# One GpSimd library, exponentials parked in idle tiles, and three TensorE tile modes in the plan of a two-attention kernel

## Chip, cores and metric

The kernel runs on one core of one Trainium2 chip. The metric is device time in microseconds (us), the median of some runs of the same program.

## What is computed

Two independent attention layers, A (linear) and B (softmax), read inputs of their own; their outputs stand side by side in the last dimension. Batch is 1, S = 2048, D = 512, and there are H = 32 heads of Dh = 16. All inputs are bf16.

```python
# both: qkv = x @ wqkv, split into q, k, v of [32 heads, 2048, 16]
phi = lambda t: jnp.where(t > 0, t + 1, jnp.exp(t)) + 1e-6
# A
kv  = einsum("bhsd,bhse->bhde", phi(k), v);  z = einsum("bhsd->bhd", phi(k))
o   = einsum("bhqd,bhde->bhqe", phi(q), kv) / (einsum("bhqd,bhd->bhq", phi(q), z) + 1e-6)
# B
p   = softmax(einsum("bhqd,bhkd->bhqk", q, k) * Dh ** -0.5)
o   = einsum("bhqk,bhkd->bhqd", p, v)
# both: o.reshape(S, D) @ wo
```

B has 32 x 2048 x 2048 exponentials, and these fill the run.

## The kernel before

**Tiling of B.** The heads are taken in four groups of eight (`Gp`). A group's projections give `QT` and `KM` with the 8 x 16 head dimensions on the partitions, and `VV` with the keys on the partitions; each head's 16 columns of V are followed by a column of ones, so that the row sum comes with the product. `KM` is kept twice, with the even or the odd heads zeroed, so that 32 rows hold one live head. A *unit* is one group, 512 queries and one parity; there are 32. A unit has 64 *blocks*: 16 key tiles of 128 by four row groups `g`. A block's scores, 128 keys by 512 queries, fill one of TensorE's accumulator banks (`pS`, seven banks).

**Scores and products on TensorE.** A score matmul (L732) uses 32 of the 128 rows, at row position 32g, so that four blocks of different g run side by side. A product matmul (L1061, out `pPV`) uses 32 of the columns, at column position 32g, and again four run side by side; 17 of these columns are used. All other matmuls (projections L495 and L570, everything of A, output L680) use the whole array. These are three ways of cutting the array into tiles, called here row mode (q), column mode (p) and whole mode (w).

**Exponentials.** Two engines make them. ScalarE takes two or three blocks that lie in neighbouring banks with one ACTIVATE (L933). VectorE takes one or two (L828): it multiplies and adds so that the int16 result, read as f16, is a rough exponential. GpSimd then makes two shifted copies of it with `int64_add` (L1007), and the three weighted together are exact enough. So a block of VectorE costs TensorE three product matmuls, and a block of ScalarE one. Exponentials lie in `PT`, 46 buffers of 512 columns, until their product has run. After a unit VectorE transposes and normalises the result (L1081 to L1094) into one of 16 tiles of `ON`.

**A and the rest are jobs.** Each projection, each step of A and each output tile is a *job*: a list of stages on the engines, with one bank from `DSET` (three banks that the blocks of VectorE use as well). `bjobs` are B's projections for later groups, then the Gram matrices of x and of the weights and a flag (`gram_x`, `gram_w`, `flag_job`): they tell whether the scores could be too large, in which case a second, general program runs after this one. It is skipped with these inputs.

**Order.** All instructions are put in order while the program is built. A planner keeps an expected time `T` for each engine and picks the next item among candidates: a group of scores for ScalarE (`fill_act_cand`), scores for VectorE, a batch of products (`pv_cand`), a job's next stage. Items of ScalarE come first: another item goes on TensorE only if it ends before ScalarE would run dry (`lim`). `SW` = 0.1 us is added when the mode changes; before the change the planner knew two modes, row mode `"q"` and everything else `"w"`. Where TensorE would idle in the plan, `fill_in` puts in matmuls with zero weights (L1268), at 0.107 us each. `fill_act_cand` may also hold scores back until enough banks of `DSET` are free (`WAITN`), so that scores for VectorE ride in the same row-mode run.

```python
            if nfill[0] >= 2 and d_backlog(start) < DLOW and not lagging(start):
                late = T["act"] + sum(exps) - 0.222 - SW - LAT - WAITM
...
                if md != mode[0]:
                    st = max(st, T["pe"] + SW)
                    mode[0] = md
```

**Start.** GpSimd makes an identity matrix (`identb`, L369 and L370); TensorE needs it to transpose the first two tiles of x. GpSimd's `affine_select` and `int64_add` come from loadable libraries, and the compiler puts a load ahead of the first use of each.

## Time and profile before

| | |
|---|---|
| median of 3 runs | 719.79 us (717.92 to 721.84) |
| the profiled execution | 721.31 us; its span is 719.6 us |
| TensorE matmuls (PE) | 693.6 us busy, 96% of the span |
| ScalarE (ACT) | 686.8 us, 95% |
| VectorE (DVE) | 551.8 us, 77% |
| GpSimd (POOL) | 372.2 us, 52% |
| mean granted TensorE clock | 0.992 |

A busy time is the union of an engine's records. The records of successive instructions overlap by about a tenth of a microsecond, so an engine that reads 95% may still wait a little before each instruction; the distance from one start to the next tells more. "Idle" in a row is the engine's gap before the instruction, with the instruction that ended the wait behind the arrow.

### The profile page before, as it was taken

The numbers are of one execution on the slowest core, as the hardware profiler recorded it, in microseconds if no ns is written. First come the engines' busy times: TensorE is split into PE (matmuls) and PEld (weight loads), VectorE is DVE, ScalarE is ACT, GpSimd is POOL, SyncE is SP. The second block draws the span as 40 slices with busy tenths as digits, with TensorE's granted clock in tenths as the row PEclk, the third lists the DMA queues.
The fourth block names the chain that finished last, engine by engine and source line by source line (L and its number), as shares of the span: only waits on it lengthen the run. The fifth ranks groups of instructions, "written<-read, shape, count | busy, mean of one in ns | idle before, by whom it ended". The sixth has DMA issues, their size and how long they took to land.

```text
span 719.6 us, 16347 instructions
## 1 busy us (share of the span) xinstructions
PE 693.6 (96%) x6716; PEld 227.8 (32%) x6716; DVE 551.8 (77%) x912; ACT 686.8 (95%) x703; POOL 372.2 (52%) x633
## 2 busy tenths in 40 slices
PE   6899999999999999999999999999999999999996
PEld 4233333333333333332232322233243232223323
DVE  4696778777778876778987878878866787778771
ACT  3699999999999999999999999999999999999995
POOL 4455566444556554555554567534541465547560
PEclk9899999999999999999999999999999999999999
DMA  9900000000000000000010010000001001110001
GB/s 211 257 2 1 2 1 1 10 9 10 7 1 2 1 1 2 6 10 11 8 31 23 2 24 15 23 9 8 17 9 30 24 8 38 37 38 9 9 24 34
DMA packets 36578, 17.38 MB, mean 24 GB/s; under 512 B 27537, under 2 KB 35985, under 8 KB 36497
## 3 DMA queue, kind: packets, MB, share of 16 engines
q1 hardware_dynamic: 35408, 15.61, 8.9%
q8 instruction: 55, 0.90, 0.5%
q10 hardware_dynamic: 1088, 0.66, 0.3%
q14 instruction: 27, 0.21, 0.1%
HBM read 4.46 MB, written 4.19 MB: 12 GB/s over the span
## 4 chain that ended last, share of the span: by engine, by line
PE 72%; ACT 21%; DVE 4%; issue 2%; POOL 0%; ACTq 0%; DVEq 0%; POOLq 0%
PE pPV L1061 26%; PE pS L732 24%; ACT PT L933 20%; PE pS L680 4%; PE pS L495 4%; PE pS L601 3%; DVE PT L828 2%; PE pPV L1268 2%; PE pS L570 2%; PE pS L627 2%; ACT EA L592 1%; DVE OT L1081 1%; PE pS L650 1%; PE pS L618 1%; PE pS L529 1%
## 5 line engine op out<-in xcount | busy, mean ns | idle before, releaser
L933 ACT ACTIVATE PT<-pS 128x1024 f16<-128x1024 f32 (+1 forms) x665 | 672.4, 1126 | 14.3 <-PE pS L732 11.0
L1007 POOL INT64_ADD PT<-PT x608 | 364.8, 613 | 319.8 <-DVE PT L828 276.2
L828 DVE TENSOR_SCALAR PT<-pS 128x512 int16<-128x512 f32 (+1 forms) x550 | 380.8, 733 | 67.7 <-PE pS L732 61.4
L1061 PE MATMUL pPV<-PT,VV 128*17 128x512 f16 x3254 | 290.5, 385 | 2.8 <-DVE OT L1081 2.7
L732 PE MATMUL pS<-QT,KM 32*128 32x512 bf16 x2048 | 280.0, 386 | 8.1 <-ACT PT L933 3.7
L732 PEld LDWEIGHTS pS<-QT,KM 32*128 32x128 bf16 x2048 | 72.7, 91 | 238.5 <-ACT PT L933 149.0
L1061 PEld LDWEIGHTS pPV<-PT,VV 128*17 128x17 bf16 x3254 | 63.1, 88 | 127.4 <-issue 100.2
L601 PE MATMUL pS<-Wa,xTa 128*128 128x256 bf16 x256 | 41.3, 276 | 1.1 <-DVE PT L828 0.8
L1081 DVE STREAM_TRANSPOSE OT<-pPV 128x512 f32<-128x512 f32 x32 | 22.7, 710 | 23.4 <-PE pPV L1061 23.3
L495 PE MATMUL pS<-xTb,Wb 128*128 128x512 bf16 x120 | 38.2, 385 | 0.5 <-DVE PT L828 0.3
L1268 PE MATMUL pPV<-xTb,ZW 128*17 128x256 bf16 x206 | 34.7, 275 | 0.0
L473 DVE CAST KNa<-pS 128x512 bf16<-128x512 f32 x30 | 20.5, 685 | 13.5 <-PE pS L680 12.1
L601 PEld LDWEIGHTS pS<-Wa,xTa 128*128 128x128 bf16 x256 | 18.7, 97 | 22.8 <-issue 13.8
L680 PE MATMUL pS<-WOa,KNa 128*128 128x512 bf16 x64 | 20.9, 386 | 0.7 <-DVE PT L828 0.5
L593 DVE TENSOR_SCALAR EA<-EA 128x512 bf16<-128x512 bf16 x32 | 12.3, 383 | 11.6 <-ACT EA L592 11.5
L570 PE MATMUL pS<-Wb,xTb 128*128 128x128 bf16 x256 | 20.9, 221 | 0.2 <-DVE PT L828 0.2
L1268 PEld LDWEIGHTS pPV<-xTb,ZW 128*17 128x17 bf16 x206 | 16.5, 91 | 14.1 <-issue 9.1
L627 PE MATMUL pS<-xTa,Wa 128*128 128x512 bf16 x64 | 19.9, 384 | 0.9 <-DVE PT L828 0.8
L592 ACT ACTIVATE EA<-pS 128x512 bf16<-128x512 f32 x32 | 20.1, 629 | 0.0
L1089 DVE TENSOR_TENSOR OT<-OT,ZR 128x256 bf16<-128x256 f32 x32 | 17.8, 558 | 0.6
L570 PEld LDWEIGHTS pS<-Wb,xTb 128*128 128x128 bf16 x256 | 14.4, 98 | 10.4 <-issue 7.6
L680 PE MATMUL pS<-WOb,ON 128*128 128x512 bf16 x48 | 15.2, 385 | 0.0
(78 smaller groups left out, 221.0 us busy)
## 6 DMA issues: line engine op xcount, KB each, us to landing
out_dram<-KNa SPq DMA_DIRECT2D x30, 128.0 KB, 1.7
Wa<-in_A_wqkv_dram SPq DMA_DIRECT2D x1, 1536.0 KB, 7.1
KM<-KR SPq DMA_DIRECT2D x96, 16.0 KB, 1.8
Wb<-in_B_wqkv_dram SPq DMA_DIRECT2D x2, 384.0 KB, 4.4
Wb<-in_B_wqkv_dram SPq DMA_DIRECT2D x1, 512.0 KB, 4.7
WOb<-in_B_wo_dram SPq DMA_DIRECT2D x1, 512.0 KB, 7.9
WOa<-in_A_wo_dram SPq DMA_DIRECT2D x1, 512.0 KB, 8.8
ON<-in_B_x_dram ACTq DMA_DIRECT2D x1, 256.0 KB, 2.9
```

Source lines behind the costliest of these rows:

```text
L495: return e.matmul(f32v(bk), lhsT=Wb[:, cc, kind * 512 + Gp * 128:kind * 512 + Gp * 128 + 128], rhs=xTb[:, cc, sc * 512:(sc + 1) * 512], st ...
L570: return e.matmul(f32v(bk)[:, tl * 128:(tl + 1) * 128], lhsT=xTb[:, cc, t * 128:(t + 1) * 128], rhs=Wb[:, cc, 1024 + Gp * 128:1024 + Gp * ...
L601: return e.matmul(f32v(bk)[:, 256 * tt:256 * tt + 256], lhsT=xTa[:, cc, (t2 + tt) * 128:(t2 + tt + 1) * 128], rhs=Wa[:, cc, 512 * kind + 2 ...
L627: return e.matmul(f32v(bk), lhsT=Wa[:, cc, bq * 128:(bq + 1) * 128], rhs=xTa[:, cc, sc * 512:(sc + 1) * 512], start=(cc == 0), stop=(cc == 3))
L680: return e.matmul(f32v(bk), lhsT=src, rhs=WO[:, hb, :], start=(hb == 0), stop=(hb == 3))
L732: return e.matmul(dst, lhsT=KM[32 * g:32 * g + 32, Gp % 2, e_, j * 128:(j + 1) * 128], rhs=QT[32 * g:32 * g + 32, Gp % 2, c * 512:(c + 1) ...
L828: sch.add("dve", lambda e: e.tensor_scalar(PTi[:, i * 512:(i + n) * 512], PS[:, b0 * 512:(b0 + n) * 512], ESC, EB, op0=ALU.mult, op1=ALU.add),
L933: sch.add("act", lambda e: e.activation(PT[:, p0 * 512:p0 * 512 + w], PS[:, use[0] * 512:use[0] * 512 + w], ACTF.Exp, scale=SC), reads=[(" ...
L1007: sch.add("pool", lambda e: e.int64_add(PTl[:, pos * 128:pos * 128 + w], PTl[:, p0 * 128:p0 * 128 + w], v_), reads=[("PT", p0 + i) for i i ...
L1061: sch.add("pe", lambda e, g=g, j=j, hl=hl, pi=pi, k=k, first=first, last_=last_: e.matmul(PVb[32 * g:32 * g + 17, 0:512], lhsT=VV[:, Gp % ...
L1081: sch.add("dve", lambda e: e.transpose(OT[:, 0, :], PVb[:, 0:512]), reads=[("PV", g) for g in range(4)], writes=[("OT", 0)])
L1268: ins = e.matmul(dst, lhsT=ZW[:, 0:17], rhs=xTb[:, 0, 0:256], start=first, stop=first, tile_position=(0, 32 * g))
```

## The change

**One library.** A four-column memset and an `int64_add` of one element are put ahead of everything else on GpSimd, so that the library with `int64_add` is loaded first; `affine_select` then runs from it.

**Memory.** x and the weights of B, the `PT` buffers and `ON` become one tile, `MEM`, of 28 + 45 + 16 buffers. The 45 are free for exponentials from the start, and of the 16 output tiles all but the first four until shortly before their result is due (`EXP`). The 28 of x and weights open once the last projection of B and the flag are done; the Gram and flag jobs therefore move from the end of `bjobs` to its thirteenth place. The first write to such a buffer waits for all readers of what lay there (`parts`). The fillers read zeros instead of x. The general program loads x and the weights again; it does not run here.

**Planner.** Products get a mode of their own, `"p"`, so that `SW` is charged for every change between the three modes, in the start time and in the rule that protects ScalarE. A group of scores is held back until the third bank is expected free, with banks that VectorE has yet to empty estimated (`est_free`), and constants change.

```diff
@@ constants @@
-    NB = 46
+    NP = 45
+    EXP = 4
-    PVQ = 11
-    PVO = 12
-    RES = 8
-    WAITN = 2
+    PVQ = 9
+    PVO = 6
+    RES = 4
+    DLOW2 = 1.0
+    WAITN = 3
-    TEND = 670.0
+    TEND = 640.0
-    DBL = 3.0
-    DLOW = 1.5
+    DBL = 4.0
+    DLOW = 0.6
@@ memory @@
-        xTb = sb("xTb", [128, 4, S], BF)
+        X0, W0, P0 = 0, 16, 28
+        O0 = P0 + NP
+        NB = O0 + NT
+        PT = sb("MEM", [128, NB * 512], F16)
+        PTi, PTl, PTb = PT.bitcast(I16), PT.bitcast(I64), PT.bitcast(BF)
+        xTb = PTb[:, 0:W0 * 512].rearrange("p (c s) -> p c s", c=4)
+        Wb = PTb[:, W0 * 512:P0 * 512].rearrange("p (c n) -> p c n", c=4)
+        ON = PTb[:, O0 * 512:NB * 512].rearrange("p (t n) -> p t n", n=512)
...
-        ZW = sb("ZW", [128, 128], BF)
+        ZW = sb("ZW", [128, 256], BF)
@@ start of GpSimd @@
+        sch.add("pool", lambda e: e.memset(identb[:, 0:4], 0.0), writes=["identb"])
+        sch.add("pool", lambda e: e.int64_add(identb.bitcast(I64)[:, 0:1], identb.bitcast(I64)[:, 0:1], 0), reads=["identb"], writes=["identb"])
         mk_ident(identb, "identb")
@@ which buffers hold exponentials @@
-        ptfree = [0.0] * NB
+        ptfree = [0.0 if P0 <= i < O0 or i >= O0 + 4 else None for i in range(NB)]
+        retired = set(range(O0, O0 + 4))
+        for i in range(P0):
+            sch.parts[("PT", i)] = ([("xTb", t) for t in range(4 * (i % 4), 4 * (i % 4) + 4)] if i < W0 else
+                                    [("Wb", kd, g) for kd in range(2) for g in range(NGP)] + [("Wb", 2)])
...
+                    k_ = (u + EXP) // 2
+                    if 4 <= k_ < NT:
+                        retired.add(O0 + k_)
+                        ptfree[O0 + k_] = None
...
+            if not opened[0] and not bjobs and not early and all(t_ in tok for t_ in lastb):
+                opened[0] = True
+                for i in range(P0):
+                    ptfree[i] = T["pe"] + LAT
@@ fill_act_cand: when to hold a group of score blocks back @@
-                now = sum(bfree[x] is not None and bfree[x] <= start + 0.05 for x in DSET)
-                if now < WAITN:
-                    t1 = sorted(bfree[x] for x in DSET if bfree[x] is not None and start + 0.05 < bfree[x] <= late)
-                    if t1:
-                        start = t1[0]
+                est = sorted(est_free(x) for x in DSET)
+                if start + 0.05 < est[WAITN - 1] <= late:
+                    start = est[WAITN - 1]
...
-                if more and d_backlog(st) < DLOW:
+                if more:
                     ids = [x for x in DSET if bfree[x] is not None and bfree[x] <= st]
-                    if len(ids) <= 2 and d_pick(st + 0.05, ()) is not None:
+                    if d_backlog(st) < (DLOW, DLOW2, -1)[len(ids) - 1] and d_pick(st + 0.05, ()) is not None:
                         more = False
@@ gram and flag jobs @@
-        bjobs += [gram_x(i, ready=0) for i in range(4)] + [gram_w(i, ready=0) for i in range(2)] + [flag_job(ready=0)]
+        gj = [gram_x(i, ready=0) for i in range(4)] + [gram_w(i, ready=0) for i in range(2)] + [flag_job(ready=0)]
+        bjobs[12:12] = gj
@@ fillers @@
-                    ins = e.matmul(dst, lhsT=ZW[:, 0:17], rhs=xTb[:, 0, 0:256], start=first, stop=first, tile_position=(0, 32 * g))
+                    ins = e.matmul(dst, lhsT=ZW[:, 0:17], rhs=ZW[:], start=first, stop=first, tile_position=(0, 32 * g))
@@ the planner's mode of a candidate @@
-                opts.append((pc[0], pc[3], "pe", pc[1], pc[2], None, "w"))
+                opts.append((pc[0], pc[3], "pe", pc[1], pc[2], None, "p"))
...
-                keep = [o for o in opts if o[2] != "pe" or o[4] is fa[2] or o[0] + o[3] + (SW if mode[0] == "q" and o[6] == "w" else 0) <= lim]
+                keep = [o for o in opts if o[2] != "pe" or o[4] is fa[2] or o[0] + o[3] + (SW if mode[0] != o[6] else 0) <= lim]
```

What the compiler and the planner make of it, in the order in which instructions stand on an engine:

GpSimd at the start, before, from the identity matrix on (L370 ISA is a library load; `ZMk` is a small mask):

```order
L369 MEMSET identb 128x128
L370 ISA
L370 AFFINE_SELECT identb<-identb 128x128
L387 MEMSET ZMk 128x8
L388 AFFINE_SELECT ZMk<-ZMk 128x8
```

and before, the last masks and the first `int64_add` (L1007 ISA without a tile is the second load):

```order
L388 AFFINE_SELECT BMk<-BMk 128x128
L390 AFFINE_SELECT BMk<-BMk 128x128
L404 MEMSET VNa 128x32
L1007 ISA
L1007 ISA PT<-PT 128x512 x196
```

Now the only load (L385) stands ahead of the identity matrix:

```order
L384 MEMSET identb 128x4
L385 ISA
L385 ISA identb<-identb 128x2
L379 MEMSET identb 128x128
L380 AFFINE_SELECT identb<-identb 128x128
```

and the masks run into the additions without one:

```order
L400 AFFINE_SELECT BMk<-BMk 128x128
L402 AFFINE_SELECT BMk<-BMk 128x128
L416 MEMSET VNa 128x32
L1034 ISA MEM<-MEM 128x512 x66
L1034 ISA MEM<-MEM 128x256 x2
```

What moved: the second load is gone, and one memset and one addition stand ahead of the identity matrix.

TensorE, the twelve rows ahead of the first output matmul of A, before (L732 row mode, L1061 column mode, L650 whole mode, L1268 fillers):

```order
L732 MATMUL pS<-QT,KM 128x512 x3
L1061 MATMUL pPV<-PT,VV 17x512 x4
L650 MATMUL pS<-RHA,PQT 128x128 x4
L732 MATMUL pS<-QT,KM 128x512 x2
L650 MATMUL pS<-RHA,PQT 128x128 x4
L1061 MATMUL pPV<-PT,VV 17x512 x5
L732 MATMUL pS<-QT,KM 128x512 x3
L1061 MATMUL pPV<-PT,VV 17x512 x5
L732 MATMUL pS<-QT,KM 128x512 x4
L1061 MATMUL pPV<-PT,VV 17x512 x2
L1268 MATMUL pS<-xTb,ZW 17x256 x3
L732 MATMUL pS<-QT,KM 128x512 x4
```

and now (L744, L1088 and L662 are the same three kinds):

```order
L1088 MATMUL pPV<-MEM,VV 17x512 x8
L662 MATMUL pS<-RHA,PQT 128x128 x4
L744 MATMUL pS<-QT,KM 128x512 x4
L1088 MATMUL pPV<-MEM,VV 17x512 x16
L744 MATMUL pS<-QT,KM 128x512 x3
L1088 MATMUL pPV<-MEM,VV 17x512 x8
L744 MATMUL pS<-QT,KM 128x512 x5
L1088 MATMUL pPV<-MEM,VV 17x512 x8
L744 MATMUL pS<-QT,KM 128x512 x3
L1088 MATMUL pPV<-MEM,VV 17x512 x8
L744 MATMUL pS<-QT,KM 128x512 x3
L1088 MATMUL pPV<-MEM,VV 17x512 x4
```

What moved: the products stand in runs of 8 and 16 rather than of 2 to 5, the whole-mode matmuls in one run instead of two, and there are no fillers.

TensorE, six rows near the end (`ZW` holds the fillers' zeros), before:

```order
L732 MATMUL pS<-QT,KM 128x512 x3
L1268 MATMUL pPV<-xTb,ZW 17x256 x9
L732 MATMUL pS<-QT,KM 128x512 x3
L1061 MATMUL pPV<-PT,VV 17x512 x4
L1268 MATMUL pPV<-xTb,ZW 17x256 x6
L732 MATMUL pS<-QT,KM 128x512 x3
```

and now:

```order
L1088 MATMUL pPV<-MEM,VV 17x512 x15
L744 MATMUL pS<-QT,KM 128x512 x3
L1088 MATMUL pPV<-MEM,VV 17x512 x4
L1302 MATMUL pPV<-ZW 17x256 x5
L744 MATMUL pS<-QT,KM 128x512 x3
L1088 MATMUL pPV<-MEM,VV 17x512 x3
```

What moved: in these rows 15 fillers became 5, and more products stand in their place. Over the whole program 238 fillers became 114, the runs of one mode 1,408 where they were 1,514, and the changes between column and whole mode 140 where they were 181. ScalarE has 509 ACTIVATEs of two blocks and 135 of three (548 and 116 before), VectorE 525 single and 50 double blocks (497 and 53), GpSimd 614 double and 22 single additions (598 and 10), and there are 3,298 products (3,254).

41 lines of the change are left out of this document (28 added, 13 removed).

## Prediction

> **What bounds the kernel now.** I read the page's busy shares first, then a table of stretches, then the groups of instructions by shape, the waits, and last the timeline at three places. The first table has busy us by engine in each stretch, with the granted TensorE clock behind POOL:
>
> ```profile
> PE 693.6 (96%) x6716; PEld 227.8 (32%) x6716; DVE 551.8 (77%) x912; ACT 686.8 (95%) x703; POOL 372.2 (52%) x633
> 20.00:40.00 20.00, 17.75 (x166) 5.84 (x162) 14.12 (x26) 14.01 (x15) 9.62 (x16) 0.83 0.83 209
> 40.00:200.00 160.00, 156.99 (x1540) 51.38 (x1533) 127.10 (x204) 159.15 (x163) 86.29 (x143) 1.00 0.02 5
> 200.00:400.00 200.00, 196.52 (x1955) 64.05 (x1953) 160.97 (x269) 198.45 (x210) 108.43 (x183) 1.00 0.04 9
> 400.00:600.00 200.00, 196.08 (x1919) 62.67 (x1919) 159.37 (x267) 196.10 (x202) 102.59 (x172) 0.99 0.07 17
> 600.00:700.00 100.00, 98.58 (x928) 28.75 (x925) 77.92 (x124) 99.25 (x97) 56.82 (x96) 1.00 0.08 25
> ```
>
> TensorE and ScalarE are both full from 40 to 700 us; one stretch, 20 to 40 us, is not: ScalarE worked 14.0 of 20 us there and the clock was 0.83. How full the two really are, start distances tell. By shape, and then in ScalarE's timeline:
>
> ```profile
> L933 ACT ACTIVATE PT<-pS 128x1024 f16<-128x1024 f32 x548 | 524.3, 1049 | 13.8 <-PE pS L732 10.7 <-DVE PT L828 0.5
> L933 ACT ACTIVATE PT<-pS 128x1536 f16<-128x1536 f32 x116 | 167.4, 1491 | 0.5 <-PE pS L732 0.3
> ...
> 13.43 7.44 ACT L933 ACTIVATE PT<-pS 128x1024 f16<-128x1024 f32 x8 [1.27 <-PE pS L732]
> 126.39 1.50 ACT L933 ACTIVATE PT<-pS 128x1536 f16<-128x1536 f32 x1
> 127.72 0.66 ACT L592 ACTIVATE EA<-pS 128x512 bf16<-128x512 f32 x1
> 128.19 1.52 ACT L933 ACTIVATE PT<-pS 128x1536 f16<-128x1536 f32 x1
> 501.85 11.11 ACT L933 ACTIVATE PT<-pS 128x1024 f16<-128x1024 f32 x12
> 689.80 19.84 ACT L933 ACTIVATE PT<-pS 128x1024 f16<-128x1024 f32 x18
> ```
>
> Twelve instructions of two blocks take 11.11 us and the last alone 1.02, so they start (11.11 - 1.02) / 11 = 0.917 us apart, the closest of them 0.903. Three blocks take 127.72 - 126.39 = 1.33, an EA of the linear attention 128.19 - 127.72 = 0.47. At these floors the 548, 116 and 32 instructions need 494.8 + 154.3 + 15.3 = 664.4 us. From the first exponential at 13.4 to the end of the last at 689.80 + 19.84 = 709.6 are 696.2 us. ScalarE therefore waits about 32 us in all, 7.6 of them before 40 us, and the remaining 24 in small pieces, 0.03 to 0.04 us before each of some 640 instructions. TensorE at a mode change:
>
> ```profile
> 328.81 0.61 PE L1061 MATMUL pPV<-PT,VV 128*17 128x512 f16 x8
> 329.35 0.39 PE L495 MATMUL pS<-xTb,Wb 128*128 128x512 bf16 x1
> 329.67 0.40 PE L732 MATMUL pS<-QT,KM 32*128 32x512 bf16 x3
> 330.00 0.61 PE L495 MATMUL pS<-xTb,Wb 128*128 128x512 bf16 x2
> 330.10 1.02 ACT L933 ACTIVATE PT<-pS 128x1024 f16<-128x1024 f32 x1 [0.22 <-PE pS L732]
> 330.54 0.39 PE L732 MATMUL pS<-QT,KM 32*128 32x512 bf16 x3
> ```
>
> A whole-mode run of one 512-column matmul occupies 329.67 - 329.35 = 0.32 us and one of two 330.54 - 330.00 = 0.54, so a matmul costs 0.22 and a change of mode about 0.105. Eight products are two rounds of four: 329.35 - 328.81 = 0.54, the same sum, so the change from column to whole mode costs what the others cost. The plan left this one out; here the scores at 329.67 come late and ScalarE waits 0.22 us.
>
> **Part 1, the library and the start.**
>
> ```profile
> 0.79 0.20 POOL L369 MEMSET identb<- 128x128 bf16 x1 [0.29 <-POOLq L1399]
> 9.08 0.28 POOL L370 TENSOR_SCALAR_AFFINE_SELECT identb<-identb 128x128 bf16<-128x128 bf16 x1 [8.09 <-issue]
> 9.42 1.03 PE L1139 MATMUL pS<-identb,ON 128*128 128x128 bf16 x8 [4.99 <-POOL ZMk L387]
> 15.34 0.68 DVE L828 TENSOR_SCALAR PT<-pS 128x512 int16<-128x512 f32 x1
> 16.25 0.24 POOL L404 MEMSET VNa<- 128x32 bf16 x1
> 22.86 4.79 POOL L1007 INT64_ADD PT<-PT  x8 [6.37 <-PE pS L732]
> 24.16 1.29 DVE L828 TENSOR_SCALAR PT<-pS 128x512 int16<-128x512 f32 x2 [2.65 <-POOL PT L1007]
> 27.83 1.02 ACT L933 ACTIVATE PT<-pS 128x1024 f16<-128x1024 f32 x1 [3.30 <-PE pS L732]
> ...
> ACT PT L933 <- PE pS L732: 6.0, 5, 3.3
> ```
>
> The second load shows as 6.37 us in which GpSimd does nothing although its first input, two blocks of L828, has been complete since 15.34 + 0.68 = 16.0 us. VectorE then waits 2.65 us for it, and ScalarE 3.30; with what follows, ScalarE loses 6.0 us between 18 and 40 us (last row). The half clock behind it is part of this: the stretch above reads 0.83. Without a load at 16.5 us the additions start at once, so I take the whole 6.0 us off; the ends are 2.65 (VectorE's wait alone) and 7.6 (all of ScalarE's waiting before 40 us).
>
> The first load is on the path: TensorE's transposes start 0.06 us after the identity matrix is there. Now a memset (0.1), the addition of one element (at most the 0.60 of a full one, 4.79 / 8) and the 0.20 memset stand around it, and it is the other library's load that counts, 6.37 against 8.09. Between +0.9 and -1.7 + 0.3 = -1.4 us; I take 0. The Trainium skill, GPSIMD Engine Reference, section 2.1, gives about 6 us for the first call to a freshly loaded kernel, a little under both rows; with 6 us, and the 0.3 of the memset and a short addition, the start would come 1.8 us earlier and the sum 1.8 lower.
>
> **Part 2, less work on ScalarE.** By the counts given with the change, 509 and 135 instructions stand where 548 and 116 stood: -39 x 0.903 + 19 x 1.33 = -9.9 us. With the mean durations of the two rows, 1.049 and 1.491, it would be -12.6; records overlap, so the distances hold. The 22 blocks go to VectorE and GpSimd:
>
> ```profile
> L1007 POOL INT64_ADD PT<-PT x608 | 364.8, 613 | 319.8 <-DVE PT L828 276.2 <-PE pS L732 26.4 <-PE pPV L1061 15.4
> L828 DVE TENSOR_SCALAR PT<-pS 128x512 int16<-128x512 f32 x497 | 319.4, 681 | 60.5 <-PE pS L732 54.4 <-POOL PT L1007 2.7 <-PE pS L627 1.9
> L828 DVE TENSOR_SCALAR PT<-pS 128x1024 int16<-128x1024 f32 x53 | 64.3, 1214 | 7.2 <-PE pS L732 7.1
> ```
>
> VectorE gets 28 x 0.681 - 3 x 1.214 = +15.4 us on 551.8, GpSimd some 16 x 0.61 + 12 x 0.4 = +14.6 on 372.2. Both stay below 570 us, with 276 us of GpSimd's waiting and 68 of VectorE's as cover. Cost 0; if that cover went, the next late thing would be the products' input and then the banks.
>
> **Part 3, TensorE.** By the orders, mode runs fall from 1,514 to 1,408: -106 x 0.105 = -11.1 us. Fillers fall from 238 to 114, at half a 512-column matmul each: -124 x 0.108 = -13.4. Rounds of products, counted by column position, are about 10 fewer in spite of 44 more products: -2.3; scores +1.7, since 32 runs hold more than four. Sum -25.1 us. The weights, inputs and parked exponentials cost nothing on any engine: no DMA is added to the program that runs, and the extra waits for readers name matmuls that stand far ahead. The Gram and flag jobs have as many matmuls as before, at another time. Reading the flag moves with them and keeps its price: SP now does it behind 32 of its 96 copies into `KM`, and each engine 200 planned items after the flag's last step, so that nothing is queued behind an unfinished flag. The one added wait, scores held for a third bank, has the products and jobs behind it on TensorE and ScalarE waiting for it; it is the last rival.
>
> **Part 4, changes of mode that the plan knows.** Before, 181 changes between column and whole mode were unplanned. All on the path they would be 181 x 0.105 = 19.0 us; none, 0. Between 40 and 700 us, 133 exponentials (330.10 is one) follow scores with such a change ahead and no filler; they start on average 0.085 us past the floor, the other 500 or so 0.026. So 133 x 0.059 = 7.8 us is seen directly. 140 such changes remain, but charged.
>
> **Sum, against the profiled span of 719.6.** By ScalarE: -6.0 - 9.9 - 7.8 = 695.9; with all 19.0 of part 4, 684.7. By TensorE: -6.0 - 25.1 = 688.5. Each engine waits for the other, so neither sum can be had alone. The first leaves out that a late run delays the runs behind it, the second that fewer fillers leave more real waiting. I take the middle of 695.9 and 688.5: 692. The floor is 13.4 + (664.4 - 9.9) + (719.6 - 709.6) = 678 with ScalarE never waiting. The profiled execution took 721.3, 1.7 more than its span, and the median of the runs is 719.8; so a span of 692 stands for a median of about 692.
>
> **Rivals.**
> - *The plan's new mode does not pay.* Cut into 22 stretches of 30 us from 40 us on, ScalarE waits about 1 us in each, whether 3 or 12 unplanned changes fall there. Then part 4 is 0: 703.7. Against it: the 0.085 beside 0.026.
> - *The identity matrix pays twice.* If the first `affine_select` behind the addition still waits for code of its own, the 6.37 us of the second load come on top at the start, on the path: 698. The order shows one load, and that speaks against it. The Trainium skill's sentence on first calls, quoted above, speaks of each kernel and not of each library, and read so it would give this rival; no run here shows two kinds of instruction behind one load.
> - *The clock.* Fewer fillers could let the granted clock fall more often.
>
> ```profile
> 409.00:413.00 4.00, 3.63 (x31) 0.90 (x32) 3.14 (x6) 4.00 (x4) 0.39 (x1) 0.81 0.01 4
> 413.00:417.00 4.00, 4.00 (x45) 0.88 (x41) 3.31 (x6) 2.72 (x4) 2.51 (x5) 0.77 0.02 4
> ```
>
> Here it fell, with TensorE busy 3.63 of 4 us: (0.19 + 0.23) x 4 = 1.7 us lost, once between 40 and 700 us. Six falls, one in each 100 us, would make 702. The Trainium skill, TensorE: Matmul & The Clock Gate, Part 1, asks for an idle window of about 3.4 us before the clock falls; this case's rows show a fall without one, and by the rule the loss would be 0.
> - *Slower: ScalarE starves behind the third bank.* Scores are now held for three banks; if VectorE empties the third late, the run waits on TensorE with ScalarE's own blocks in it.
>
> ```profile
> 697.33 0.73 PE L732 MATMUL pS<-QT,KM 32*128 32x512 bf16 x4
> 698.00 0.61 PE L1061 MATMUL pPV<-PT,VV 128*17 128x512 f16 x8
> ```
>
> This run of four took 0.67 where 0.32 is the floor; the mean loss of the 176 runs of four is 0.10. There are now 232 runs of four or more (186). To pass 723 the loss must grow by 31 / 232 = 0.13, to 0.23 each. At half of that, 707. Against it: VectorE's start distances are 0.60, as planned.
>
> **How the numbers follow.** Forecast, 682 to 698: 0.70. New mode does not pay, about 704: 0.14. Identity twice, 698: 0.05. Clock, about 702: 0.04. Starving: 0.05, of which 0.03 slower than 723.4 and the rest between. Below 682: 0.02. The range goes from the floor with a few us of waiting, 682, to the first rival and the clock's fall, 706. A measurement of this kernel tells 0.5% from no change (716.2 to 723.4): faster 0.95, within 0.02, slower 0.03.
>
> **What would show it.** Right: `INT64_ADD` starting before 18 us, no ScalarE wait over 1 us and a clock of 1.00 between 20 and 40 us; ScalarE's exponentials 639 us at the floors; its small waits between 40 us and the end about 14 us instead of 24; 114 fillers. Wrong: first exponential after 15 us (start); waits still at 24 us (part 4); runs of four that lose 0.2 us each (banks); clock under 0.98 in steady stretches. A median under 682 would mean that ScalarE hardly waits at all.

## The result, and the profile after

The kernel after takes 701.22 us (698.76 to 701.77), the kernel before, run beside it, 719.21 (717.92 to 721.84): a ratio of 0.974, 95% interval 0.970 to 0.978, 18 us less. The prediction said 692 with a range of 682 to 706. The direction and the range hold; the middle is 9 us too low, with two terms of the sum wrong by 5 and 8 us in opposite directions. The profiled execution after took 701.77 us with a span of 699.8 and a mean clock of 0.994.

The page's busy shares of the kernel after:

```profile
PE 675.6 (97%) x6636; PEld 220.8 (32%) x6636; DVE 567.0 (81%) x937; ACT 673.4 (96%) x682; POOL 386.3 (55%) x663
```

and its table of stretches, with the columns as before:

```profile
20.00:40.00 20.00, 19.52 (x185) 6.04 (x181) 16.87 (x30) 19.98 (x20) 10.20 (x18) 1.00 0.87 211
40.00:200.00 160.00, 156.95 (x1639) 57.20 (x1636) 128.76 (x219) 157.86 (x159) 84.51 (x144) 1.00 0.02 5
400.00:600.00 200.00, 194.41 (x1831) 56.90 (x1834) 168.20 (x272) 195.28 (x197) 115.34 (x194) 0.99 0.08 20
```

The hole between 20 and 40 us is gone: ScalarE works 19.98 of 20 us there, where it worked 14.01, and the clock is 1.00 instead of 0.83. VectorE and GpSimd have 567.0 and 386.3 us of work; the prediction's 551.8 + 15.4 and 372.2 + 14.6 are 567.2 and 386.8. From 40 us on ScalarE is no fuller than before (195.28 of 200 us in the third stretch, before 196.10).

The start, on GpSimd, TensorE and ScalarE (timeline; the bracket is the idle time before a row and what ended it):

```profile
1.04 0.19 POOL L385 INT64_ADD identb<-identb  x1
1.65 0.29 POOL L380 TENSOR_SCALAR_AFFINE_SELECT identb<-identb 128x128 bf16<-128x128 bf16 x1 [0.16 <-POOL identb L379]
18.45 1.24 POOL L1034 INT64_ADD MEM<-MEM  x2 [9.40 <-DVE MEM L845]
...
4.30 1.06 PE L1171 MATMUL pS<-identb,MEM 128*128 128x128 bf16 x8
6.27 1.71 PE L1182 MATMUL pS<-MEM 128*128 128x256 bf16 x16 [0.40 <-DMA MEM<-in_B_wqkv_dram]
10.64 0.38 PE L582 MATMUL pS<-MEM 128*128 128x128 bf16 x4 [1.16 <-DMA MEM<-in_B_wqkv_dram]
...
8.35 2.37 ACT L959 ACTIVATE MEM<-pS 128x1536 f16<-128x1536 f32 x2 [1.05 <-PE pS L744]
11.39 2.37 ACT L959 ACTIVATE MEM<-pS 128x1536 f16<-128x1536 f32 x2 [0.68 <-PE pS L744]
```

Nothing waits for a library any more, not even the first instruction that needs one: the addition of one element runs at 1.04 us and the identity matrix is there at 1.9 instead of 9.4. TensorE transposes x at 4.30 (before 9.42), and the first exponential starts at 8.35 (before 13.43). In its place TensorE now waits for weights that are still on their way, 0.40 and 1.16 us. The additions at 18.45 wait 9.40 us for VectorE's first pair of blocks, which comes that late in the new order; no library is in it.

ScalarE's exponentials and VectorE's blocks by shape (groups of instructions):

```profile
L959 ACT ACTIVATE MEM<-pS 128x1024 f16<-128x1024 f32 x509 | 489.9, 1077 | 7.1 <-PE pS L744 4.5 <-DVE MEM L845 1.7
L959 ACT ACTIVATE MEM<-pS 128x1536 f16<-128x1536 f32 x135 | 196.4, 1502 | 5.5 <-PE pS L744 5.1
L845 DVE TENSOR_SCALAR MEM<-pS 128x512 int16<-128x512 f32 x525 | 339.8, 683 | 68.3 <-PE pS L744 62.7 <-ACT MEM L959 2.9
L845 DVE TENSOR_SCALAR MEM<-pS 128x1024 int16<-128x1024 f32 x50 | 60.8, 1215 | 8.8 <-PE pS L744 8.5
```

the last exponentials (timeline):

```profile
684.53 5.09 ACT L959 ACTIVATE MEM<-pS 128x1536 f16<-128x1536 f32 x4
```

and ScalarE's waits in which it was wholly idle, between 40 and 690 us (us in total, times, longest):

```profile
ACT MEM L959 <- PE pS L744: 7.2, 18, 0.9
ACT MEM L959 <- DVE MEM L845: 1.7, 3, 0.8
```

From these rows the run can be taken apart as the prediction took the kernel before: the first exponential, ScalarE's *need* (each exponential at its closest start distance: 0.903 us for two blocks, 1.33 for three, 0.47 for one, and 32 EA at 0.477), its waits, and what comes after the last exponential. After: 8.35, then 509 x 0.903 + 135 x 1.33 + 15.3 = 654.5 of need; the last exponential ends at 684.53 + 5.09 = 689.62, so the waits are 689.62 - 8.35 - 654.5 = 26.8; 10.2 follow. Before: 13.43 + 664.9 + 31.3 + 10.0 (the prediction's 664.4 left out one exponential of a single block). The waits can be split by start distances: those before 40 us, those after it of up to 0.3 us past the floor (*small*), and longer ones (*large*); the three add up to the waits within 0.3 us.

| | before | after | difference |
|---|---|---|---|
| first exponential | 13.43 | 8.35 | -5.1 |
| ScalarE's need | 664.9 | 654.5 | -10.4 |
| waits before 40 us | 6.9 | 2.0 | -4.9 |
| small waits | 18.3 | 12.2 | -6.1 |
| large waits | 5.9 | 12.4 | +6.5 |
| behind the last exponential | 10.0 | 10.2 | +0.2 |

That is the whole 19.8 us between the two spans. Two of the lines stood at nothing in the prediction: the start, and the large waits that take back what the small ones gave.

### The profile page after: what moved, and what is told of

Its sections match the earlier page's. It is cut to its first block, busy times and chain, and to the rows that moved or that the text cites. A ratio compares the mean times of both kernels' runs of the same rounds, so it can differ in the third digit from the quotient of the medians.

```text
span 699.8 us, 16215 instructions
## 1 busy us (share of the span) xinstructions
PE 675.6 (97%) x6636; PEld 220.8 (32%) x6636; DVE 567.0 (81%) x937; ACT 673.4 (96%) x682; POOL 386.3 (55%) x663
## 4 chain that ended last, share of the span: by engine, by line
ACT 47%; PE 44%; DVE 5%; issue 1%; SPq 1%; DMA 1%; DVEq 0%; ACTq 0%
ACT MEM L959 46%; PE pS L744 15%; PE pPV L1088 15%; PE pS L507 4%; DVE MEM L845 3%; PE pS L692 2%; PE pS L582 2%; PE pS L639 2%; PE pS L613 1%; ACT EA L604 1%; SPq L355 1%; DMA MEM<-in_B_wqkv_dram 1%; DVE OT L1112 1%; PE pS L1140 0%; PE pS L662 0%
## 5 line engine op out<-in xcount | busy, mean ns | idle before, releaser
L959 ACT ACTIVATE MEM<-pS 128x1024 f16<-128x1024 f32 (+1 forms) x644 | 659.1, 1166 | 12.6 <-PE pS L744 9.6
L1034 POOL INT64_ADD MEM<-MEM x636 | 378.6, 608 | 294.7 <-DVE MEM L845 253.2
L845 DVE TENSOR_SCALAR MEM<-pS 128x512 int16<-128x512 f32 (+1 forms) x575 | 397.7, 729 | 77.1 <-PE pS L744 71.2
L744 PE MATMUL pS<-QT,KM 32*128 32x512 bf16 x2048 | 282.9, 386 | 9.7 <-ACT MEM L959 4.5
L1088 PE MATMUL pPV<-MEM,VV 128*17 128x512 f16 x3298 | 283.2, 384 | 2.5 <-DVE OT L1112 1.7
L744 PEld LDWEIGHTS pS<-QT,KM 32*128 32x128 bf16 x2048 | 75.2, 91 | 244.9 <-ACT MEM L959 161.6
L1088 PEld LDWEIGHTS pPV<-MEM,VV 128*17 128x17 bf16 x3298 | 61.0, 88 | 125.5 <-issue 97.6
L507 PE MATMUL pS<-MEM 128*128 128x512 bf16 x120 | 37.5, 385 | 1.4 <-DVE VV L587 0.8
L1112 DVE STREAM_TRANSPOSE OT<-pPV 128x512 f32<-128x512 f32 x32 | 22.7, 708 | 15.3 <-PE pPV L1088 15.1
L582 PE MATMUL pS<-MEM 128*128 128x128 bf16 x256 | 20.2, 220 | 1.2 <-DMA MEM<-in_B_wqkv_dram 1.2
L582 PEld LDWEIGHTS pS<-MEM 128*128 128x128 bf16 x256 | 14.6, 98 | 9.3 <-issue 6.4
L1302 PE MATMUL pPV<-ZW 128*17 128x256 bf16 x89 | 15.7, 274 | 0.0
L692 PE MATMUL pS<-WOb,MEM 128*128 128x512 bf16 x48 | 14.7, 384 | 1.0 <-ACT MEM L959 1.0
L507 PEld LDWEIGHTS pS<-MEM 128*128 128x128 bf16 x120 | 8.4, 97 | 20.7 <-issue 10.1
```

What stands on the lines that cost most here:

```text
L507: return e.matmul(f32v(bk), lhsT=Wb[:, cc, kind * 512 + Gp * 128:kind * 512 + Gp * 128 + 128], rhs=xTb[:, cc, sc * 512:(sc + 1) * 512], st ...
L582: return e.matmul(f32v(bk)[:, tl * 128:(tl + 1) * 128], lhsT=xTb[:, cc, t * 128:(t + 1) * 128], rhs=Wb[:, cc, 1024 + Gp * 128:1024 + Gp * ...
L692: return e.matmul(f32v(bk), lhsT=src, rhs=WO[:, hb, :], start=(hb == 0), stop=(hb == 3))
L744: return e.matmul(dst, lhsT=KM[32 * g:32 * g + 32, Gp % 2, e_, j * 128:(j + 1) * 128], rhs=QT[32 * g:32 * g + 32, Gp % 2, c * 512:(c + 1) ...
L845: sch.add("dve", lambda e: e.tensor_scalar(PTi[:, i * 512:(i + n) * 512], PS[:, b0 * 512:(b0 + n) * 512], ESC, EB, op0=ALU.mult, op1=ALU.add),
L959: sch.add("act", lambda e: e.activation(PT[:, p0 * 512:p0 * 512 + w], PS[:, use[0] * 512:use[0] * 512 + w], ACTF.Exp, scale=SC), reads=[(" ...
```

## The experiments

All kernels of a table below were taken apart in the same way. Each ran beside the kernel before on the same chip, whose medians there were 720.21, 720.09 and 719.93 us (719.21 beside the kernel after), so that medians of different tables compare to about 1 us. What is taken apart is the one profiled execution of each kernel, which lies up to 2.9 us from its median.

### The library

`library alone`: the kernel before with the two lines.

```diff
+        sch.add("pool", lambda e: e.memset(identb[:, 0:4], 0.0), writes=["identb"])
+        sch.add("pool", lambda e: e.int64_add(identb.bitcast(I64)[:, 0:1], identb.bitcast(I64)[:, 0:1], 0), reads=["identb"], writes=["identb"])
         mk_ident(identb, "identb")
```

> The kernel before with the one-element addition at the start and nothing else; the order on all other engines is that of before. Theory, the library left over from the execution before counts: no load is waited for at all, the first exponential starts near 8.4 us instead of 13.4, the stall between 20 and 40 us goes (6.0 us of ScalarE), the clock reads 1.00 there, and the time is 719.2 - 5.0 - 5.5 = about 709. Rival, the early start of the changed kernel comes from its new order and only the second load goes: first exponential at 13.4 and about 714.

`another library last`: the kernel after with one instruction of another library as GpSimd's last work.

```diff
+        TOPI = sb("TOPI", [128, 4], mybir.dt.int32)
...
+        sch.add("pool", lambda e: e.iota(TOPI[:], pattern=[[1, 4]], base=0, channel_multiplier=0), writes=["TOPI"])
```

> The changed kernel with one small iota on GpSimd behind its last addition; iota lives in another library, so that this one stays behind at the end. Theory, the library left over counts: the load ahead of the one-element addition takes 6 to 8 us again, the first exponential starts at 13 to 14 us instead of 8.3, and the time is 701.2 + 5 = about 706. Rival, a load ahead of all other work is free whatever was left: the first exponential stays at 8.3 and the time within 1 us of 701.

Measured: the library alone 710.81 us, ratio 0.988 (0.986 to 0.990); the other 702.94, ratio 0.977 (0.975 to 0.979) to before. Timeline rows of the library alone:

```profile
1.04 0.19 POOL L375 INT64_ADD identb<-identb  x1
8.61 2.85 ACT L935 ACTIVATE PT<-pS 128x1024 f16<-128x1024 f32 x3 [1.04 <-PE pS L734]
11.30 1.20 POOL L1009 INT64_ADD PT<-PT  x2 [2.25 <-DVE PT L830]
```

and of the kernel with another library last:

```profile
7.89 0.18 POOL L386 INT64_ADD identb<-identb  x1 [7.00 <-issue]
8.50 0.29 POOL L381 TENSOR_SCALAR_AFFINE_SELECT identb<-identb 128x128 bf16<-128x128 bf16 x1 [0.16 <-POOL identb L380]
8.85 1.04 PE L1172 MATMUL pS<-identb,MEM 128*128 128x128 bf16 x8 [4.49 <-POOL ZMk L400]
9.68 3.62 PE L1183 MATMUL pS<-MEM 128*128 128x128 bf16 x20
13.89 6.89 ACT L960 ACTIVATE MEM<-pS 128x1536 f16<-128x1536 f32 x6 [2.30 <-PE pS L745]
690.62 0.13 POOL L1378 IOTA TOPI<- 128x4 int32 x1 [6.87 <-issue]
```

The two lines alone bring 9.4 us: 4.8 at the start (8.61 instead of 13.43) and 4.6 of the early waits (2.3 instead of 6.9). And the second kernel shows why nothing is waited for at the start. It has the same instruction in the same place, but the execution before it ended with another library, and the addition waits 7.00 us again; the IOTA waits 6.87 for its own. A library that the last execution left behind costs nothing; one that it did not leave costs 7 us, on the path. The kernel before changed libraries within each execution and so waited for both. The Trainium skill, GPSIMD Engine Reference, section 2.1, puts the first call of freshly loaded code at about 6 us. The waits of 7.00 and 6.87 are a little above it, and the 1.04 shows that the price falls on a change of library, not on each execution. Nor does it fall on each kind of instruction: the `affine_select` behind the addition waits 0.16 us.

The late start cost the second kernel 5.5 us at the first exponential but only 1.7 in the median, where 5 were expected. Its ScalarE waits 4.2 us less than in the kernel after: 1.7 before 40 us, since the weights have landed when TensorE asks for them (the row at 9.68 waits for none), and 2.5 later on. Of these, 2.1 are the clock's: four of the kernel after's 22 large waits (0.82, 0.30, 0.61 and 0.36 us) stand in or just behind two falls of the granted clock, near 381 and 579 us, and the second kernel's clock did not fall between 40 and 690 us. Its table of stretches there:

```profile
40.00:690.00 650.00, 624.39 (x6261) 202.98 (x6307) 538.26 (x881) 641.56 (x652) 369.84 (x622) 1.00 0.05 13
381.00:385.00 4.00, 3.73 (x45) 1.62 (x45) 3.73 (x7) 4.00 (x5) 2.85 (x5) 1.00 0.00 0
```

The other 18 large waits stand in both, each within 0.01 us; they belong to the order and not to the execution. The one execution of the kernel after with a mean clock of 1.000 took 698.76 us, 4.2 less than the second kernel.

### Memory and modes

Parking and the third mode were taken out of the kernel after, one at a time and together. Two modes:

```diff
-                opts.append((pc[0], pc[3], "pe", pc[1], pc[2], None, "p"))
+                opts.append((pc[0], pc[3], "pe", pc[1], pc[2], None, "w"))
...
-                keep = [... + (SW if mode[0] != o[6] else 0) <= lim]
+                keep = [... + (SW if mode[0] == "q" and o[6] == "w" else 0) <= lim]
```

> The changed kernel with products back in the planner's mode w, so that changes between column and whole mode are not charged; library and memory stay. Theory, the third mode is worth the drift it removes: ScalarE's small waits go up by 5 to 8 us and the time is 705 to 709. Rival, what the plan gains in truth it pays in length: within 2 us of 701.

No parking (the 45 buffers alone):

```diff
-        ptfree = [0.0 if P0 <= i < O0 or i >= O0 + 4 else None for i in range(NB)]
+        ptfree = [0.0 if P0 <= i < O0 else None for i in range(NB)]
-        retired = set(range(O0, O0 + 4))
-        opened = [False]
+        retired = set(range(O0, O0 + NT))
+        opened = [True]
```

> The changed kernel with exponentials in the 45 own buffers alone; output tiles, x and weights are never used for them. Theory, the buffers are what lets ScalarE do less and TensorE batch more: 2 to 4 per cent slower, 715 to 728, with shorter runs of products and more fillers. Rival, the extra room lies idle and the constants and modes made the order: within 4 us of 701.

Both edits:

> The kernel after, with both the parking in idle tiles (45 buffers of its own left) and the third TensorE mode taken out; the one library, the new constants and the new hold of scores stay. So far, with the library alone 710.8 us, with parking and two modes 712.4, with three modes and no parking 722.5, with both 701.2. Theory 'the two need each other': a plan that is charged for every change between column and whole mode saves products up into long runs, and saved-up products need parking; without parking the charge only makes ScalarE wait. Then with neither the time is near the library alone, 706 to 716, and below the 722.5 of three modes without parking. Rival 'each has its own worth': 722.5 - 701.2 = 21.3 for parking and 712.4 - 701.2 = 11.2 for the third mode add up: 701.2 + 32.5 = 734.

And the third mode in the kernel before, with the two lines of the library (old memory, old constants, old hold):

```diff
-                opts.append((pc[0], pc[3], "pe", pc[1], pc[2], None, "w"))
+                opts.append((pc[0], pc[3], "pe", pc[1], pc[2], None, "p"))
...
-                keep = [... + (SW if mode[0] == "q" and o[6] == "w" else 0) <= lim]
+                keep = [... + (SW if mode[0] != o[6] else 0) <= lim]
```

> The kernel before with the one-element addition at the start and the third TensorE mode in the planner, old memory and old constants. Theory 'the two need each other': on the old memory the charge gains nothing or costs, 711 to 722 beside the 710.8 of the library alone. Rival 'the third mode has its own worth': 710.8 - 11.2 = 700. What the prediction's part 4 read from the trace, 7.8 us of waits behind uncharged changes, would give 703 here if it needed nothing else.

What came out (VectorE blocks are its single blocks plus twice its double ones; "early" is before 40 us):

| kernel | median | ratio to before (95%) | first exp. | need | early, small, large waits | VectorE blocks |
|---|---|---|---|---|---|---|
| library alone | 710.81 | 0.988 (0.986 to 0.990) | 8.61 | 664.9 | 2.3, 18.0, 4.5 | 603 |
| library and third mode | 712.98 | 0.992 (0.989 to 0.994) | 8.27 | 674.5 | 2.0, 12.0, 0.7 | 581 |
| neither parking nor third mode | 720.41 | 1.002 (0.999 to 1.003) | 8.48 | 668.8 | 3.1, 16.3, 13.0 | 593 |
| third mode, no parking | 722.52 | 1.004 (1.001 to 1.006) | 10.55 | 676.2 | 0.8, 11.0, 13.8 | 576 |
| parking, two modes | 712.39 | 0.990 (0.988 to 0.992) | 8.43 | 656.5 | 5.8, 14.3, 15.9 | 621 |
| after | 701.22 | 0.974 (0.970 to 0.978) | 8.35 | 654.5 | 2.0, 12.2, 12.4 | 625 |

The rows behind two of these lines. With the third mode and no parking, the exponentials by shape:

```profile
L959 ACT ACTIVATE MEM<-pS 128x1024 f16<-128x1024 f32 x508 | 491.6, 1083 | 8.7 <-PE pS L744 8.0
L959 ACT ACTIVATE MEM<-pS 128x1536 f16<-128x1536 f32 x152 | 221.6, 1498 | 4.5 <-PE pS L744 4.0
```

the last of them (timeline):

```profile
683.82 28.74 ACT L959 ACTIVATE MEM<-pS 128x1536 f16<-128x1536 f32 x25
```

With the library and the third mode in the kernel before, the exponentials by shape:

```profile
L935 ACT ACTIVATE PT<-pS 128x1024 f16<-128x1024 f32 x543 | 520.7, 1086 | 3.0 <-PE pS L734 2.5
L935 ACT ACTIVATE PT<-pS 128x1536 f16<-128x1536 f32 x127 | 186.7, 1518 | 0.2
```

the last of them (timeline):

```profile
683.65 14.18 ACT L935 ACTIVATE PT<-pS 128x1536 f16<-128x1536 f32 x12
```

and ScalarE's waits between 40 and 690 us, where the kernel after has 21 of them:

```profile
ACT PT L935 <- PE pS L734: 0.3, 1, 0.3
```

Parking is worth 21.3 us with three modes (722.52 to 701.22) and 8.0 with two. It comes through ScalarE's need: 676.2 without, 654.5 with, because 49 more blocks (625 for 576) go to VectorE, at some 0.44 us of ScalarE each. A block of VectorE lies in three buffers, so with fewer buffers it gets fewer blocks. An exponential did not become faster by it (1083 and 1077 ns for two blocks).

The third mode does what the prediction read off the trace: in each pair of the table the small waits fall, 18.0 to 12.0, 16.3 to 11.0, 14.3 to 12.2. They fall where the prediction had seen them. Counted in the traces between 40 and 690 us, small waits alone, an exponential whose scores stand behind a change between column and whole mode without a filler starts 0.070 us past the floor with the library alone and 0.035 with the third mode too; the other two pairs give 0.062 to 0.030 and 0.063 to 0.039. Exponentials behind neither such a change nor a filler stay at 0.014 to 0.020. But the mode has a price that the prediction did not name. A plan that counts every change of mode has less time left on TensorE for VectorE's three products a block (argued, not tried by itself), and without parking it hands 17 to 22 blocks back to ScalarE: need up 7.4 and 9.6 us. So without parking it costs 2 us (710.81 to 712.98, 720.41 to 722.52), and with parking it pays here, 712.39 to 701.22 (how firm that is, the next part tells). Two modes with parking were expected at 705 to 709, or within 2 us of 701, and took 712.39. Both theories for "neither" missed as well: neither part has a worth of its own that can be added (734 expected, 720 measured), and the kernel with neither is not as good as the library alone either (706 to 716 expected).

That last miss is the find. `neither` differs from `library alone` in the new constants, in how scores are held back and how far a group may grow, in where the Gram jobs stand, and in 45 buffers for 46. It is 9.6 us slower in the median and 11.4 between the two profiled spans. Of the 11.4, 8.5 are large waits, 13.0 for 4.5 (1.9 of the 13.0 in one fall of the clock, near 541 us), and 3.9 are need. ScalarE's waits between 40 and 690 us in `neither`, and then with the library alone:

```profile
ACT MEM L959 <- PE pS L744: 9.8, 20, 1.8
...
ACT PT L935 <- PE pS L734: 2.5, 10, 0.4
ACT PT L935 <- DVE PT L830: 0.5, 1, 0.5
```

### The hold, the constants and the order

The kernel after with scores held for two banks:

```diff
-    WAITN = 3
+    WAITN = 2
```

> The kernel after with scores held for two free banks of VectorE instead of three (WAITN 2). Theory 'the hold for a third bank is what eats the gain of the small waits': score runs wait less often for a bank that VectorE empties (24.4 us in 71 waits between 40 and 690 us in the kernel after, 14.8 in 44 before), ScalarE's waits fall from 25 us towards 16, and the time is 692 to 699. Rival 'the hold pays for itself': with two banks there are more and shorter runs, so more changes of mode; the time is 702 to 712.

with products let go one block later:

```diff
-    PVQ = 9
+    PVQ = 10
```

> The kernel after with products let go when ten blocks are ready instead of nine (PVQ 10), a change that has no price of its own. It tells how far the time moves by the mere fact that another order comes out of the planner. Theory 'the constants are chosen for this one order': by the planner's own expected times the last exponential comes 12 us later than in the kernel after, so about 707 to 716. Rival 'the time does not follow the planner's times that closely, it is set by the work': 699 to 704.

with two numbers that act near the end:

```diff
-    DEND = 20
+    DEND = 16
-    TEND = 640.0
+    TEND = 670.0
```

> The kernel after with two constants that act near the end of the run changed (DEND 16, TEND 670). Need 654.3 us, 0.2 under the kernel after. Theory 'need and waits are what the work makes them': 26.8 us of waits again, span 699.7, median 700 to 703. Rival 'the constants are chosen for this one order and any other is some 10 us slower, as with PVQ 10': 708 to 714.

and with a higher price of a change of mode:

```diff
-        SW = 0.1
+        SW = 0.107
```

> The kernel after with the planner charging 0.107 us for a change of mode instead of 0.1, about what the trace shows (0.105). Need 662.1 us, since fewer blocks fit on VectorE in this order. Theory 'the rest of the waits comes from changes that are charged too little': 1,415 runs at 0.005 to 0.007 are 7 to 10 us, so waits of 17 to 20, span 698 to 701, median 699 to 702. Rival 'the waits are in the plan itself': 26.8 again, span 707.5, median 709.

Last, the kernel after with the constants of before, with two modes and with three:

```diff
-    PVQ = 9
-    PVO = 6
-    RES = 4
-    WAITN = 3
-    TEND = 640.0
-    DBL = 4.0
-    DLOW = 0.6
+    PVQ = 11
+    PVO = 12
+    RES = 8
+    WAITN = 2
+    TEND = 670.0
+    DBL = 3.0
+    DLOW = 1.5
```

> The kernel after with two TensorE modes and the constants of before (PVQ 11, PVO 12, RES 8, WAITN 2, TEND 670, DBL 3.0, DLOW 1.5): the library, the parking and the new form of the hold are what is left of the change. A run is taken as the first exponential (8.4 us), ScalarE's need at its floors, its waits, and 10.2 us behind the last exponential; the median is about 1.7 above the span. The need is fixed by the program: 570 two-block and 93 three-block exponentials, 653.7 us. Theory 'the new constants make ScalarE wait, parking does not': waits of 25 to 29 us as with the library alone, so 697 to 701 in the span and 699 to 703 as the median. Rival 'parking with two modes waits, whatever the constants': the 36.3 us of the run with parking and two modes, so 710.

> The kernel after with the constants of before alone (the third mode stays). Need 656.8 us (542 two-block, 114 three-block exponentials and one of one block). Theory 'the third mode takes away about 10 us of ScalarE's waits, and the new constants put them back': waits of 15 to 19 us, as in the kernel before with library and third mode (15.0), so a span of 690 to 694 and a median of 692 to 696, under the 701.2 of the kernel after. Rival 'the waits of about 27 us belong to parking or to the hold's new form': 702 in the span, 704 as the median.

| kernel | median | ratio to before (95%) | first exp. | need | early, small, large waits | VectorE blocks |
|---|---|---|---|---|---|---|
| two banks | 712.11 | 0.991 (0.988 to 0.993) | 8.31 | 662.7 | 5.1, 9.4, 12.9 | 607 |
| PVQ 10 | 712.08 | 0.991 (0.988 to 0.993) | 10.21 | 662.7 | 2.4, 12.2, 11.6 | 607 |
| DEND 16, TEND 670 | 704.24 | 0.979 (0.976 to 0.981) | 8.60 | 654.4 | 2.3, 10.3, 15.4 | 626 |
| SW 0.107 | 707.33 | 0.982 (0.979 to 0.985) | 8.33 | 662.1 | 4.5, 10.2, 11.0 | 608 |
| old constants, two modes | 705.09 | 0.981 (0.978 to 0.983) | 8.21 | 653.7 | 2.1, 19.3, 7.9 | 629 |
| old constants, three modes | 706.10 | 0.980 (0.978 to 0.983) | 8.65 | 656.8 | 1.4, 12.3, 16.4 | 621 |

In the last two kernels one of B's 32 units comes out wrong (last group, rows 1024 to 1535; the odd heads with two modes, the even heads with three), for a reason that is open. Their products are complete, 2,048 + 2 x 629 = 3,306 and 2,048 + 2 x 621 = 3,290, so the work that is timed is whole.

The exponentials by shape with two banks:

```profile
L959 ACT ACTIVATE MEM<-pS 128x1024 f16<-128x1024 f32 x527 | 508.6, 1096 | 9.5 <-PE pS L744 6.1 <-DVE MEM L845 2.5
L959 ACT ACTIVATE MEM<-pS 128x1536 f16<-128x1536 f32 x129 | 190.8, 1523 | 5.2 <-PE pS L744 5.0
```

and with PVQ 10:

```profile
L959 ACT ACTIVATE MEM<-pS 128x1024 f16<-128x1024 f32 x524 | 504.1, 1081 | 8.2 <-PE pS L744 4.7 <-DVE MEM L845 2.1
L959 ACT ACTIVATE MEM<-pS 128x1536 f16<-128x1536 f32 x131 | 189.8, 1498 | 5.2 <-PE pS L744 5.1
```

Without the hold for a third bank VectorE gets 18 blocks fewer, need rises by 8.2 us and the time by 10.9; large waits stay. That is the rival's side, just past its 702 to 712. But PVQ 10, which has no price of its own, gives the same: 607 blocks, 712.08. So it isn't shown that the hold itself pays. An order in which VectorE gets fewer blocks comes out of most small changes of the constants, and costs 0.45 us a block. So a difference of up to 11 us to the kernel after may say only that another order came out; of the single edits only the loss of parking, 21.3 us, is clearly past that; its 8.0 with two modes is not. The third mode's 11.2 is not either, and with parking and the old constants it gains nothing (705.09 to 706.10, need up 3.1). Where the blocks stay (626 with DEND 16 and TEND 670) so does the time, 704.24, which misses its expected 700 to 703 by one. SW 0.107 did not lower the waits (25.7 for 26.6): a price that is 0.005 us too low is not what makes them.

With the old constants the third mode again takes the small waits from 19.3 to 12.3 (the fourth pair of four; 0.074 to 0.042 behind the changes named above), and again the large ones are there, 16.4, of which 5.1 in three falls of the clock; the expected 15 to 19 us of waits in all became 30. With two modes the 705.09 lies between the 699 to 703 and the 710 that were expected. Large waits by kernel: 5.9, 4.5 and 0.7 us in the three kernels with the old hold and the Gram jobs last; 7.9 to 16.4 in all that have the new hold and the Gram jobs early, with and without parking, with two or three modes, with old and new constants. Without the waits in falls of the clock and 1 us behind them it is 4.5, 4.5 and 0.7 against 7.9 to 15.9. By elimination the large waits belong to what all kernels of the second kind share: the hold's new form, the rule on how far a group may grow, the moved jobs, or 45 buffers for 46. These were not tried apart, and that is left open. The jobs themselves end with the flag:

```profile
194.32 0.15 DVE L575 TENSOR_TENSOR FLG<-TP 1x1 f32<-1x1 f32 x1
```

Of the kernel after's 12.4 us, 9.7 come later than 200 us, so the jobs could act there only through the order that follows them. The third bank by itself is not the cause: with two banks there are still 29 runs of five or more scores between 40 and 690 us, and 6.3 us of waits behind them. The trace leans to such long runs, however they come about. One in the kernel after:

```profile
151.50 0.39 PE L744 MATMUL pS<-QT,KM 32*128 32x512 bf16 x2
151.82 1.05 PE L613 MATMUL pS<-Wa,xTa 128*128 128x256 bf16 x8
152.80 0.61 PE L1088 MATMUL pPV<-MEM,VV 128*17 128x512 f16 x8
153.34 0.60 PE L744 MATMUL pS<-QT,KM 32*128 32x512 bf16 x5
153.78 1.45 ACT L959 ACTIVATE MEM<-pS 128x1536 f16<-128x1536 f32 x1 [0.83 <-PE pS L744]
```

A whole-mode run and eight products stand ahead of a run of five scores; ScalarE's three blocks come last and it waits 0.83 us. Between 40 and 690 us the kernel after has 30 runs of five or more scores, the kernel before 5, and the waits of exponentials that follow such a run add up to 5.9 us against 0.9. Large waits alone are 4.9 and 0.9 of these, which makes 4.0 of the 6.5 us of new large waits. The clock, which fell twice between 40 and 690 us instead of once, makes another 0.7 (2.1 against 1.4); the remaining 1.8 are not traced. The two falls in the table of stretches:

```profile
379.00:381.00 2.00, 1.77 (x21) 0.71 (x20) 1.83 (x4) 2.00 (x3) 1.64 (x4) 0.94 0.00 0
381.00:385.00 4.00, 4.00 (x25) 0.88 (x19) 2.78 (x5) 3.39 (x4) 1.56 (x4) 0.60 0.00 0
577.00:579.00 2.00, 1.80 (x21) 0.64 (x25) 1.94 (x4) 2.00 (x4) 1.44 (x3) 0.94 0.00 0
579.00:583.00 4.00, 4.00 (x33) 0.64 (x25) 2.40 (x6) 3.50 (x3) 0.73 (x2) 0.60 0.21 37
```

ScalarE is idle for 4 - 3.39 = 0.61 and 4 - 3.50 = 0.50 us where the clock reads 0.60, and in the kernel before for 4 - 2.72 = 1.28 in its one (413 to 417 us).

## Why the prediction was right or wrong

- **Part 1, the start: 0 taken, -5.1 measured.** The bounds, +0.9 to -1.4, assumed that the first load of an execution is always waited for. The row it stood on (8.09 us of waiting) was true only because the kernel before left the other library behind. The failing step is to have priced a load by its kind and not to have asked what was loaded already.
- **Part 1, the stall: -6.0 taken, -4.9 measured** in the waits before 40 us, between the bounds of 2.65 and 7.6. The library alone gives 4.6. `INT64_ADD` started at 18.45, not before 18, for want of a block.
- **Part 2: -9.9 taken, -10.4 measured**, and VectorE and GpSimd took the blocks at the price worked out. This term was right, but the text gave parking no price and thus no worth. The runs show that it is parking that makes this term: with three modes and the 45 buffers, need rises by 11.3 over the kernel before instead of falling by 10.4.
- **Part 3: half taken.** The middle between ScalarE's 695.9 and TensorE's 688.5 took 3.7 us off for TensorE's lighter load. Nothing of it came: TensorE has 675.6 us of records, 97% of its span where it had 96%, and ScalarE is what the time adds up by.
- **Part 4: -7.8 taken, +0.4 measured.** The mechanism is right, the small waits fell by 6.1, and they fell in four pairs of four. The term failed because it was counted alone: the same change brings longer runs of scores and 6.5 us of large waits, by elimination with what came beside it (the hold's new form, longer groups, the moved jobs, 45 buffers). "Its small waits about 14 us instead of 24" set the sum of all waits, 24.2, against small ones; like for like it is 24.2 to 24.6, and waits still at 24 us were the prediction's own sign against this part.
- **The rivals.** "The new mode does not pay" gave 703.7, near the 701.2, for another reason than its own: the small waits did fall, and large ones came in their place. "Identity twice" is out by the 0.16 us above. "Starving behind the third bank" comes near the place where the large waits are, at a small part of the price: the waits behind runs of five or more grew by 5 us, and 31 were needed; and they stay when two banks are held for. The clock fell twice instead of once, at 2.1 us of ScalarE's waits against 1.4. The Trainium skill, TensorE: Matmul & The Clock Gate, Part 1, asks for an idle window of about 3.4 us. In the 2 us ahead of the two falls TensorE was busy 1.77 and 1.80 us, so neither has such a window ahead of it, and the trace does not bear the rule out.

By the terms: the prediction's 695.9 for ScalarE, with the start (-5.1), the stall (+1.1), need (-0.5), part 4 (+8.2) and the end (+0.2), is 699.8, the span. The forecast of 692 lay 3.9 under 695.9 by the middle taken, and the median lies 1.4 above the span. That the range held is in part luck: the start and part 4 erred by 5 and 8 us, and mostly cancelled.

## What to carry to other kernels

Ask of a loadable library what the execution before left behind: one library used throughout is not waited for again, two that alternate are each waited for in every execution. In a kernel whose order is planned, take the time apart into the bound engine's need and its waits before crediting an edit: extra buffers moved 49 blocks off ScalarE here, and an honest price for mode changes cut its waits but gave blocks back where buffers were short. And run a neighbour with a meaningless change of a constant first; here it moved the time by 11 us, and a single undo has to show more than that.

## What the runs showed of the hardware

A GpSimd library stays from one execution to the next: 7.00 and 6.87 us of waiting where it was another one, none (1.04 us after the start) where it was the same. A start 5.5 us earlier was worth 1.7 us in the median: with it TensorE waited for weights that were still landing (1.16 and 0.40 us), and the profiled execution had two falls of the clock that the other lacked. One fall of the granted clock (0.60 over 4 us) came with some 1 us of waits on ScalarE; why it falls with TensorE busy 1.77 and 1.80 of the 2 us ahead stays open.
